# Attention and two MoE layers on one core: query tiles split half a step earlier, constants on a second queue, eight hidden-layer buffers instead of six

## The chip, the cores and the metric

The kernel runs on one core of one Trainium2 chip. The metric is device time in microseconds (us) of one execution; the time before is the median of three runs.

## The reference, cut to what matters

```python
scores = scale * np.matmul(q, k.transpose(0, 1, 3, 2))        # B,H,S,D = 2, 8, 576, 64
x = (np.log1p(np.abs(rel)) / psi_i)[..., None]                # rel = i - j
h = np.maximum(x @ w1 + b1, 0.0)                              # 32 hidden units
scores = scores + (h @ w2).transpose(2, 0, 1)[None]           # a bias for each head
attn = softmax(scores)
x = np.matmul(attn, v)                                        # as rows of 512, 1152 tokens
x = (x @ w_a) * (x @ w_b) @ w_out                             # first MoE block, d_ff 1536
x = (silu(x @ w_gate) * (x @ w_val)) @ w_out                  # second MoE block
```

## The kernel before, in words

The program is one stream: attention first, then the two MoE blocks, with one TensorE order written out by hand (`Pinned` keeps the matmuls in program order). A scheduler places the instructions of VectorE (DVE) and ScalarE (ACT) on their queues; which of the two engines gets a copy or a pass is settled at build time by `Share`, a running sum of estimated costs.

**The bias.** The class `Bias` makes the bias of all heads in 36 units of 16 rows. A unit has four passes (`passes`, L164): each makes a tile `hd` of up to 576 columns, relu(LW + bp), on DVE (L154) or ACT (L156). `LW` is the log table times w1; `bp` comes from the constants `cs`. `products` (L172) multiplies the four `hd` with w2 on TensorE into a bank `tp`, scales the result into a tile `bt` (L160 on DVE, L162 on ACT) and writes it to DRAM. `hd` has `HDS` buffers, so a pass may have to wait until TensorE has read the tile that had its buffer before.

**The attention.** A step is a pair of heads `p` and a block of rows `t`. The four steps of `t` = 4 come first and have one half each; the sixteen others have two halves (`b` = 0, 1) of 128 rows. Half `i` goes through three stages in three successive rounds of the loop at L472: `first(i)` makes the scores `ps` on TensorE (L319, in one PSUM tile of four banks), adds the bias and takes the maximum on DVE (`es`, L339) and the exponential on ACT (`es`, L345); `second(i-1)` transposes `es` into `ee`, copied out by ACT (L352) or DVE (L350); `third(i-2)` multiplies by the values (`pu`) and scales by the inverse sums (L408 to L411). After them stand the products of the bias units whose passes were issued at the top of the round. `MADE` (L36) says how many units a round has: eight in round 0, then 2, 1, 2, 1 and so on up to round 16. In a round with two units eight `hd` tiles are wanted.

**The query tiles.** The scores multiply in three terms, from a high part `qa` and a low part `qb` of the query tile: `split_q` (L230) makes `qa` (a cast on ACT, L212, or on DVE, L210) and then `qb` (a subtraction on DVE, L214) from `rawq`, which POOL's queue fetched earlier. Before the change the split for the next step is issued at the end of `first` of a step's last half (L451), so one half before its scores.

```python
            if 4 <= idx + 1 < len(steps) and (t == 4 or b == 1):
                heads.split_q(*steps[idx + 1])
```

**Queues.** SP's queue fetches `cs` (L138) and then `LW` (L139), later writes the bias and fetches MoE weights; POOL's queue fetches keys, queries, values and bias rows.

Of the kernel before, what the change touches and what calls it, by code (L numbers as in the profile page):

```python
# [34 lines left out]
FIRST = 4  # L35
MADE = (8, *(2, 1) * 8)  # L36
SCORED = 4
HDS, BTS, EES = 6, 6, 4


DFIX, DFAST, DSLOW = 160.0, 0.56, 1.04
# [34 lines left out]
class Activations:  # L76


    def __init__(self, pool):
        self.pool, self.late = pool, None  # L80
        self.acc = [pool.tile([P, NCC, CH], F32, tag=f"acc{c}", name=f"acc{c}") for c in range(2)]
        self.layer()
# [41 lines left out]
class Bias:  # L124
# [7 lines left out]
    def __init__(self, tc, stack, cst, lm, bias_d, heads, share):  # L132
        nc = self.nc = tc.nc
        self.tc, self.bias_d, self.share, self.pe, self.dve = tc, bias_d, share, Pinned(tc, nc.tensor), Pinned(tc, nc.vector)
        bc = self.bc = stack.enter_context(tc.tile_pool(name="bm", bufs=1, side="right"))
        cs = bc.tile([P, 214], F32, name="cs")
        LW = self.LW = bc.tile([P, S], F32, name="LW")
        nc.sync.dma_start(cs, cst)  # L138
        nc.sync.dma_start(LW, lm)  # L139
        one = bc.tile([P, 1], F32, name="one")  # L140
        nc.gpsimd.memset(one, 0.0)
        nc.scalar.activation(one, one, AF.Exp)
        W1, B1, self.W2, PS, self.RE = cs[:, 0:1], cs[:, 1:2], cs[:, 2:34], cs[:, 34:178], cs[:, 178:214]
        with tc.high_priority():
            bp = self.bp = bc.tile([P, 144], F32, name="bp")
            nc.vector.tensor_scalar(bp, PS, B1, None, op0=ALU.mult)
            ready = nc.vector.tensor_scalar(LW, LW, W1, None, op0=ALU.mult)
        heads.fetch_k(0)
        heads.fetch_first_q()
        heads.fetch_k(1)  # L150
# [151 lines left out]
def attention(ctx, tc, a4, heads, share, bias, units, bias_d, x, weights, ident):  # L302

    nc = tc.nc
    pe = units.pe
    with (
# [6 lines left out]
        def bias_rows(p, t, n):  # L313
            e = bias_d[t][:, 2 * p]
            return bass.AP(tensor=e.tensor, offset=e.offset + 15, ap=[[16 * H * BW, n // 16], [H * BW - 1, 16], [1, BW + S]])

        def scores(p, q, blocks, bt, sums):

            ka, kb = heads.got["k", p]  # L319
            qa, qb = q  # L320
            ps = ps2.tile([P, 2, 2, 512], F32, tag="big", name="ps")
            es = a4.tile([P, 2, S], F32, tag="es", name="es", bufs=3)
            for hf in range(2):
                for m, (lt, rt) in enumerate(((qa, ka), (qa, kb), (qb, ka))):
                    for j in range(2):
                        r = slice(64 * j, 64 * j + 64)
                        for n, (c0, b) in enumerate(blocks):
                            k0 = S * b + 288 * hf
                            pe.matmul(
                                ps[:, j, hf, :288], lt[r, c0 : c0 + P], rt[r, k0 : k0 + 288], start=m + n == 0, stop=m + n == len(blocks) + 1  # L330
                            )
            return ps, es, bt, sums

        def exponentials(ps, es, bt, sums, pinned):

            for j in range(2):
                nm = a4.tile([P, 1], F32, tag="nm", name="nm", bufs=4)
                least = (units.dve if pinned else nc.vector).tensor_tensor_reduce
                least(  # L339
                    out=es[:, j].rearrange("p (a j) -> p a j", a=2), in0=ps[:, j, :, :288], in1=bt[j].rearrange("p (a j) -> p a j", a=2),  # L340
                    op0=ALU.add, op1=ALU.min, scale=-0.125, scalar=3.0e38, accum_out=nm,
                )
                share.dve(S, 1.3)
                share.act(S, 190.0)
                nc.scalar.activation(es[:, j], es[:, j], AF.Exp, bias=nm, scale=-1.0, accum_out=sums[:, j : j + 1])  # L345
            return es.rearrange("p h k -> p (h k)")
# [77 lines left out]
        steps = [(p, t) for t in ORDER for p in range(H // 2)]  # L424
# [3 lines left out]
        def first(i):  # L428

            idx, p, t, b = halves[i]  # L430
            if b == 0:
                bt = a4.tile([P, BW + S], F32, tag="bias", name="bt", bufs=3)
                for r in range(1 if t < 4 else B):
                    n = P if t < 4 else 64
                    heads.queue.dma_start(bt[n * r : n * r + n], bias_rows(p, t, n))
                bt = [bt[:, BW * j : BW * j + S] for j in range(2)]
                if 0 < idx < 3:
                    heads.load_v(idx + 1, nc.sync)
                    heads.split_k(idx + 1)
                if 6 <= idx + 2 < len(steps):  # L440
                    heads.fetch_q(*steps[idx + 2])
                cells[idx] = bt, a2.tile([P, 4 if t < 4 else 2], F32, tag=f"sums{t < 4}", name="sums", bufs=3)
            bt, sums = cells[idx]
            blocks = [(P * b, b)] if t < 4 else [(64 * r, r) for r in range(B)]
            for made in range(MADE[0] if i == 0 else 1):
                if i == 0:
                    units.products(*units.passes(rest.pop(0)), bank)
                if made == SCORED * (i == 0):
                    live[i] = scores(p, heads.got["q", p, t], blocks, bt, sums[:, 2 * b : 2 * b + 2])
            live[i] = exponentials(*live[i], i == 0)  # L450
            if 4 <= idx + 1 < len(steps) and (t == 4 or b == 1):  # L451
                heads.split_q(*steps[idx + 1])

        def second(i):
# [17 lines left out]
        for i in range(len(halves) + 2):  # L472
            todo = [units.passes(rest.pop(0)) for _ in range(MADE[i] if 0 < i < len(MADE) else 0)]
            if i < len(halves):
                first(i)
            if 0 <= i - 1 < len(halves):
                second(i - 1)
            if i >= 2:
                third(i - 2)
            for unit in todo:  # L480
                units.products(*unit, bank)
            if i == len(MADE) - 1:
                bias.close()
                weights.pool = weights.pools[0] = ctx.enter_context(tc.tile_pool(name="wpa2", bufs=1, side="right"))
                weights.fetch(0, 0, 0)
                weights.fetch(0, 0, 1)
                ahead = chain(weights.words(0, 0, 0), weights.split(0, 0, 0), weights.words(0, 0, 1))
            if i > len(MADE) + 4:
                for op in islice(ahead, 1):
                    units.tc.keep_in_program_order(op)  # L490
# [230 lines left out]
```

## Time and profile before

| | us |
|---|---|
| median of 3 runs (652.32 to 652.73) | 652.34 |
| the profiled execution | 652.59 |
| its span in the trace | 650.5 |
| TensorE busy in the span | 617.5 (95%) |
| DVE busy | 535.8 (82%) |
| ACT busy | 344.6 (53%) |

The span is 2.1 us shorter than the profiled execution's own time. The busy shares are means over the whole span; attention, up to about 207.7 us, is a stage in which all three engines are busy, while in the MoE blocks ACT has little to do. The granted TensorE clock is 1.00 of full speed in all stretches.

### The profile page before, as it was taken

The page shows a single profiled execution, that of the slowest core. Times are in us where ns is not written, and L with a number is a line of the kernel's source. Part 1 is how long each engine was busy: PE and PEld are TensorE (multiplying, and loading weights), DVE is VectorE, ACT ScalarE, POOL GpSimd, SP SyncE. Part 2 cuts the span into 40 slices and gives each one's busy share as a digit, 9 for nine tenths or more (in the row PEclk, how much of TensorE's full clock was granted, in tenths as well). Part 3 has the DMA queues.
Part 4 walks back from the last instruction along what each step waited for, and adds up shares of the span by engine and source line. Part 5 has one row for each costly group of instructions (what it writes and reads, how often), then busy time and mean ns, then how long its engine had stood idle before and what let it go on. Part 6 is the DMA issues. An engine that isn't in the chain of part 4 may idle for free.

```text
span 650.5 us, 11312 instructions
## 1 busy us (share of the span) xinstructions
PE 617.5 (95%) x4470; PEld 554.9 (85%) x4470; DVE 535.8 (82%) x1033; ACT 344.6 (53%) x674; POOL 45.8 (7%) x66
## 2 busy tenths in 40 slices
PE   5879999999989989999999999999999999999997
PEld 2346565577778989999999999899999999999997
DVE  5968878778987899999899988997898988896452
ACT  5878888778786445544534332454555444433210
POOL 3210101011100000000000000450000000000000
PEclk9999999999999999999999999999999999999999
DMA  8884453573611331313313223111231313100012
GB/s 335 253 234 163 140 162 114 170 231 97 163 38 67 130 129 65 130 64 130 127 69 114 81 71 124 65 65 45 85 125 72 129 65 130 55 11 1 1 48 98
DMA packets 20996, 71.56 MB, mean 110 GB/s; under 512 B 5744, under 2 KB 7424, under 8 KB 16336
## 3 DMA queue, kind: packets, MB, share of 16 engines
q1 hardware_dynamic: 12672, 52.72, 22.5%
q0 software_dynamic: 8272, 18.13, 10.3%
q8 instruction: 35, 0.57, 0.4%
q14 instruction: 17, 0.14, 0.1%
HBM read 57.57 MB, written 13.25 MB: 109 GB/s over the span
## 4 chain that ended last, share of the span: by engine, by line
PE 77%; DVE 12%; ACT 7%; issue 2%; DMA 1%; POOL 0%; DVEq 0%; ACTq 0%; POOLq 0%
PE po L100 21%; PE pv L100 12%; PE pb L100 11%; PE tp L100 9%; PE pa L100 8%; PE pd L100 7%; PE pu L100 5%; PE ps L100 5%; ACT es L345 3%; ACT ee L352 1%; DVE es L339 1%; ACT hd L156 1%; DVE m L273 1%; DMA kr<-in_kd 1%; DVE hd L154 1%
## 5 line engine op out<-in xcount | busy, mean ns | idle before, releaser
L100 PE MATMUL po<-gh,woh 128*128 128x384 f32 x288 | 96.8, 336 | 1.4 <-DVE acc L597 1.3
L100 PE MATMUL po<-gl,woh 128*128 128x384 f32 x288 | 96.4, 335 | 1.2 <-DVE gl L532 1.2
L100 PE MATMUL po<-gh,wol 128*128 128x384 f32 x288 | 96.5, 335 | 0.0
L531 ACT CAST gh<-g 128x384 fp32r<-128x384 f32 x72 | 35.7, 514 | 85.6 <-DVE g L529 85.5
L100 PE MATMUL tp<-hd,cs 128*32 128x264 f32 (+17 forms) x352 | 49.3, 510 | 12.0 <-DVE hd L154 6.3
L339 DVE CUSTOM_DVE_ANT_0 es<-ps,bt 128x576 f32<-128x576 f32 x70 | 50.1, 753 | 10.7 <-PE ps L100 10.5
L345 ACT ACTIVATE es<-es,nm 128x576 f32<-128x576 f32 x72 | 55.8, 778 | 2.6 <-DVE nm L339 2.2
L100 PEld LDWEIGHTS po<-gh,woh 128*128 128x128 f32 x288 | 54.1, 188 | 2.3 <-DVE acc L597 2.3
L100 PEld LDWEIGHTS po<-gl,woh 128*128 128x128 f32 x288 | 54.1, 188 | 1.6 <-DVE gl L532 1.6
L100 PEld LDWEIGHTS po<-gh,wol 128*128 128x128 f32 x288 | 54.0, 188 | 0.0
L100 PE MATMUL pv<-x2h,wh 128*128 128x384 f32 x152 | 50.9, 335 | 0.0
L100 PE MATMUL pv<-x2l,wh 128*128 128x384 f32 x152 | 50.9, 335 | 0.0
L100 PE MATMUL pv<-x2h,wl 128*128 128x384 f32 x152 | 50.9, 335 | 0.0
L100 PE MATMUL tp<-ident,es 128*128 128x128 f32 x324 | 45.7, 281 | 2.5 <-ACT ee L352 1.8
L100 PE MATMUL pu<-ee,vv 128*64 128x128 f32 (+1 forms) x800 | 47.3, 267 | 0.0
L270 ACT ACTIVATE m<-raw 128x1024 f32<-128x1024 f32 x36 | 41.4, 1150 | 10.6 <-DVE wl L285 4.0
L100 PEld LDWEIGHTS tp<-hd,cs 128*32 128x32 f32 x352 | 13.9, 114 | 36.7 <-ACT hd L156 13.3
L284 ACT CAST wh<-m 128x1024 fp32r<-128x1024 f32 x24 | 25.3, 1053 | 37.0 <-PE pd L100 29.8
L273 DVE SCALAR_TENSOR_TENSOR m<-raw,m 128x1024 uint32<-128x1024 uint32 x36 | 44.5, 1238 | 0.2
L274 DVE SCALAR_TENSOR_TENSOR m<-raw,m 128x1024 uint32<-128x1024 uint32 x36 | 44.4, 1237 | 0.1
L100 PEld LDWEIGHTS pu<-ee,vv 128*64 128x64 f32 x800 | 39.3, 137 | 5.7 <-issue 5.2
L100 PEld LDWEIGHTS tp<-ident,es 128*128 128x128 f32 x324 | 34.5, 141 | 11.1 <-issue 4.8
(148 smaller groups left out, 1548.9 us busy)
## 6 DMA issues: line engine op xcount, KB each, us to landing
raw<-in_wm SPq DMA_DIRECT2D x36, 1024.0 KB, 4.8
bias_d<-bt SPq DMA_DIRECT2D x36, 295.5 KB, 5.5
bt<-bias_d POOLq DMA_DIRECT2D x16, 583.5 KB, 7.5
bt<-bias_d POOLq DMA_DIRECT2D x8, 291.8 KB, 10.2
kr<-in_kd POOLq DMA_DIRECT2D x4, 576.0 KB, 6.9
out_t<-acc SPq DMA_DIRECT2D x12, 192.0 KB, 1.9
rawq<-in_qd POOLq DMA_DIRECT2D x16, 128.0 KB, 3.0
vv<-in_vd SPq DMA_DIRECT2D x2, 640.0 KB, 7.5
```

The costliest lines, as they stand in the source:

```text
L100: return self.tc.keep_in_program_order(getattr(self.engine, name)(*args, **kwargs))
L154: self.last = self.nc.vector.tensor_scalar(dst, self.LW[:, :n], self.bp[:, m : m + 1], 0.0, op0=ALU.add, op1=ALU.max)
L156: self.nc.scalar.activation(dst, self.LW[:, :n], AF.Relu, bias=self.bp[:, m : m + 1])
L270: yield nc.scalar.activation(m, hi.bitcast(F32), AF.Abs)
L273: yield nc.vector.scalar_tensor_tensor(t, lo, 29, t, op0=ALU.logical_shift_right, op1=ALU.bitwise_or)
L274: yield nc.vector.scalar_tensor_tensor(t, hi, 0xC0000000, t, op0=ALU.bitwise_and, op1=ALU.bitwise_or)
L284: yield nc.scalar.copy(wh[:, :4], mt)
L339: least(out=es[:, j].rearrange("p (a j) -> p a j", a=2), in0=ps[:, j, :, :288], in1=bt[j].rearrange("p (a j) -> p a j", a=2), op0=ALU.add, ...
L345: nc.scalar.activation(es[:, j], es[:, j], AF.Exp, bias=nm, scale=-1.0, accum_out=sums[:, j : j + 1])
L352: nc.scalar.copy(dst, src)
L531: nc.scalar.copy(gh, g)
```

## The change

It has three parts. `split_q` of the next step is issued in `first` of a step's first half, one half earlier, and the first such split one step earlier. The fetch of `cs` goes to ACT's queue. `HDS` goes from 6 to 8.

```diff
-HDS, BTS, EES = 6, 6, 4
+HDS, BTS, EES = 8, 6, 4
...
-        nc.sync.dma_start(cs, cst)
+        nc.scalar.dma_start(cs, cst)
         nc.sync.dma_start(LW, lm)
...
             live[i] = exponentials(*live[i], i == 0)
-            if 4 <= idx + 1 < len(steps) and (t == 4 or b == 1):
+            if idx == 2:
+                heads.split_q(*steps[4])
+            if 4 <= idx < len(steps) - 1 and b == 0:
                 heads.split_q(*steps[idx + 1])
```

TensorE's, POOL's and (but for `cs`) SP's orders stay as they were. The scheduler orders DVE and ACT anew; the number of passes on each is the same (86 on DVE, 58 on ACT), and one copy of 128 columns goes from ACT to DVE. Three places follow.

The first is ACT's start: `hd` are the passes of the first units, `ka` the cast of the first keys, which has to wait for their fetch. Rows with - are of before, rows with + of the change.

```order
-L715 UNCONDITIONAL_BRANCH
+L717 UNCONDITIONAL_BRANCH
+L138 DMA cs<-in_cst 128x214
 L142 ACT_TABLE_LOAD
 L142 ACTIVATE one<-one 128x1
 L156 ACTIVATE hd<-LW,bp 128x528 x2
-L156 ACTIVATE hd<-LW,bp 128x544
+L156 ACTIVATE hd<-LW,bp 128x544 x2
 L212 CAST ka<-kr 128x1152
 L162 ACTIVATE bt<-tp,cs 128x63
-L156 ACTIVATE hd<-LW,bp 128x544
```

All four passes of the second unit (528 to 544 columns wide) now stand ahead of `ka`; the fourth stood behind it.

The second is DVE in round 5, between the two softmax pairs `es` (shown as ISA) of halves 4 and 5; the units there are 352 and 336 wide. Before:

```order
L339 ISA es,nm<-ps,bt 128x576
L339 ISA nm 128x1
L350 COPY ee<-tp 128x384
L160 TENSOR_SCALAR bt<-tp,cs 128x207
L350 COPY ee<-tp 128x384
L408 TENSOR_TENSOR acc_73<-pu,rc 128x128
L154 TENSOR_SCALAR hd<-LW,bp 128x352 x2
L411 TENSOR_TENSOR x0l<-acc_73,x0h 128x128
L154 TENSOR_SCALAR hd<-LW,bp 128x336
L160 TENSOR_SCALAR bt<-tp,cs 128x223
```

Of the change:

```order
L339 ISA es,nm<-ps,bt 128x576
L339 ISA nm 128x1
L210 CAST qa<-rawq 128x256
L160 TENSOR_SCALAR bt<-tp,cs 128x207
L350 COPY ee<-tp 128x384
L214 TENSOR_TENSOR qb<-rawq,qa 128x256
L390 COPY rc<-tp 128x128
L408 TENSOR_TENSOR acc_73<-pu,rc 128x128
L154 TENSOR_SCALAR hd<-LW,bp 128x336 x2
L411 TENSOR_TENSOR x0l<-acc_73,x0h 128x128
L154 TENSOR_SCALAR hd<-LW,bp 128x336
L160 TENSOR_SCALAR bt<-tp,cs 128x223
```

The passes of the first unit (352) have moved ahead of the earlier softmax pair, three of the second unit (336) stand in the gap, and the split of the next step's queries (`qa`, `qb`) stands there too, half a step before its use.

The third is ACT around the step whose scores start at 148.57 us, after the bias is done; `x1h` and `rw` belong to the end of a step, `m` to the first MoE weights. Before:

```order
L345 ACTIVATE es,sums<-es,nm 128x576
L352 COPY ee<-tp 128x384
L345 ACTIVATE es,sums<-es,nm 128x576
L212 CAST qa<-rawq 128x256
L410 CAST x1h<-acc_74 128x256
L383 COPY rw<-rs 128x256
L270 ACTIVATE m<-raw 128x1024
```

Of the change:

```order
L345 ACTIVATE es,sums<-es,nm 128x576 x2
L212 CAST qa<-rawq 128x256
L352 COPY ee<-tp 128x384
L345 ACTIVATE es,sums<-es,nm 128x576
L352 COPY ee<-tp 128x384
L345 ACTIVATE es,sums<-es,nm 128x576
L410 CAST x1h<-acc_74 128x256
L383 COPY rw<-rs 128x256
L270 ACTIVATE m<-raw 128x1024
```

The cast `qa` has moved ahead of the step's last pair of exponentials.

## Rows read from the trace of the kernel before

**Rows 1.** Busy time by stretch: stretch, length; busy PE, PEld, DVE, ACT, POOL; clock, DMA.
```profile
4.36:19.56 15.20, 11.41 (x80) 4.30 (x80) 11.40 (x22) 10.74 (x19) 2.23 (x4) 1.00 0.98 383
19.56:35.23 15.67, 13.29 (x107) 5.41 (x104) 14.51 (x32) 13.43 (x26) 4.31 (x7) 1.00 0.87 249
...
55.70:133.25 77.55, 71.55 (x781) 46.02 (x779) 62.12 (x178) 63.70 (x156) 8.10 (x13) 1.00 0.48 150
133.25:207.70 74.45, 69.38 (x808) 56.98 (x808) 60.82 (x170) 56.93 (x142) 7.93 (x13) 1.00 0.43 125
207.70:235.00 27.30, 25.63 (x145) 25.31 (x146) 24.07 (x36) 12.73 (x21) 0.00 (x0) 1.00 0.32 117
```

**Rows 2.** Waits, 36.7 to 133 us: engine, line, releaser, us in total, times, longest.
```profile
DVE hd L154 <- PE tp L100: 8.1, 8, 1.6
...
ACT hd L156 <- PE tp L100: 6.1, 7, 1.5
...
PE tp L100 <- ACT ee L352: 2.9, 6, 0.8
...
PE tp L100 <- ACT hd L156: 1.7, 4, 0.5
```

**Rows 3.** Waits of TensorE, 133 to 208 us, the same columns.
```profile
PE ps L100 <- ACT qa L212: 4.7, 5, 1.2
```

**Rows 4.** Timeline, the start: start us, us, engine, operation, [idle before <-releaser].
```profile
0.74 0.37 SPq L138 DMA_DIRECT2D cs<-in_cst  x1
...
1.17 0.42 SPq L139 DMA_DIRECT2D LW<-in_lm  x1
...
4.36 0.52 DVE L147 TENSOR_SCALAR LW<-LW,cs 128x576 f32<-128x576 f32 x1 [1.30 <-DMA LW<-in_lm]
...
8.67 1.15 ACT L212 CAST ka<-kr 128x1152 fp32r<-128x1152 f32 x1 [1.75 <-DMA kr<-in_kd]
...
11.87 0.50 DVE L160 TENSOR_SCALAR bt<-tp,cs 128x272 f32<-128x272 f32 x1 [0.66 <-PE tp L100]
...
14.68 0.96 DVE L214 TENSOR_TENSOR qb<-raw,qa 128x768 fp32r<-128x768 f32 x1 [1.46 <-ACT qa L212]
```

**Rows 5.** Timeline: the first softmax pair on DVE.
```profile
35.23 0.75 DVE L100 CUSTOM_DVE_ANT_0 es<-ps,bt 128x576 f32<-128x576 f32 x1
```

**Rows 6.** DMA issues of 22.1 to 22.6 us: bias rows, median us to landing.
```profile
bt<-bias_d POOLq DMA_DIRECT2D x2, 291.8 KB, 8.9
```

**Rows 7.** Timeline of TensorE: unit products of rounds 2 to 5, 15 and 16.
```profile
48.05 0.91 PE L100 MATMUL tp<-hd,cs 128*32 128x416 f32 x8
...
53.37 2.40 PE L100 MATMUL tp<-hd,cs 128*32 128x400 f32 x16
...
60.35 0.83 PE L100 MATMUL tp<-hd,cs 128*32 128x368 f32 x8
...
64.64 1.35 PE L100 MATMUL tp<-hd,cs 128*32 128x352 f32 x12
66.53 0.84 PE L100 MATMUL tp<-hd,cs 128*32 128x336 f32 x4 [0.53 <-ACT hd L156]
...
121.10 2.88 PE L100 MATMUL tp<-hd,cs 128*32 128x480 f32 x16
...
127.96 1.06 PE L100 MATMUL tp<-hd,cs 128*32 128x512 f32 x8
```

**Rows 8.** Timeline: the step whose scores start at 148.57 us.
```profile
148.13 0.39 ACT L212 CAST qa<-rawq 128x256 fp32r<-128x256 f32 x1
...
148.57 0.40 PE L100 MATMUL ps<-ka,qa 64*128 64x288 f32 x2 [0.88 <-ACT qa L212]
...
153.59 0.76 DVE L339 CUSTOM_DVE_ANT_0 es<-ps,bt 128x576 f32<-128x576 f32 x1 [1.48 <-PE ps L100]
```

**Rows 9.** Timeline of DVE, 163 to 177 us: the two rows with a wait.
```profile
163.06 0.29 DVE L408 TENSOR_TENSOR acc<-pu,rc 128x128 f32<-128x128 f32 x1 [0.47 <-PE pu L100]
...
176.60 0.76 DVE L339 CUSTOM_DVE_ANT_0 es<-ps,bt 128x576 f32<-128x576 f32 x1 [0.68 <-PE ps L100]
```

## The prediction

> **What bounds the kernel now.** I read the busy time by stretch first, then the waits, then the timeline where the waits stand. From 133 us on TensorE is the engine that is nearly full: it is busy 69.38 of 74.45 us in the last part of attention and 25.63 of 27.30 us where the MoE blocks begin [rows 1]. While the bias is made, from 55.70 to 133.25 us, it is busy 71.55 of 77.55 us, with DVE at 62.12 (80%) and ACT at 63.70 (82%) not far behind. In the start DVE sets the pace: up to the first softmax pair it is busy 11.40 of 15.20 and 14.51 of 15.67 us. So a gain can come from three places: DVE's waits in the start, TensorE's waits while the bias is made, and TensorE's waits after it. TensorE's order of work does not change, so what counts is when DVE and ACT deliver.
>
> The waits name the causes. Between 36.7 and 133 us DVE's passes `hd` waited 8 times, 8.1 us in all, until TensorE had read an older tile, and ACT's 7 times, 6.1 us [rows 2]. There are eight rounds with two units in that stretch (1, 3, ... 15), each wanting eight tiles where there are six buffers: the second unit's last passes wait for the first unit's products, and its products then wait for them. After 133 us TensorE's only frequent wait is for `qa` on ACT: 5 times, 4.7 us [rows 3].
>
> **The change, part by part.**
>
> *Constants on ACT's queue.* `LW` is issued at 1.17 us, behind `cs` at 0.74 [rows 4]; alone on SP's queue it can be issued at 0.74, so 0.43 us earlier. DVE waits for it 1.30 us after its work on `cs`, which is the most that could go; nothing goes if the transfer takes longer beside that of `cs`. I take 0.43, the issue slot, because that is the part that the rows show to be serial. ACT pays one issue ahead of its table load. I book nothing for it, since its first pass has to wait for `LW` anyway; if that cover were gone it would cost about 0.4 us (the issue of `cs` took 0.37). [...]
>
> *Eight buffers in the start.* ACT idles 1.75 us ahead of `ka` at 8.67 us, waiting for the keys [rows 4]. A fourth pass now stands in that gap, so that the second unit's products can follow the first's, and DVE's wait of 0.66 us at 11.87 for those products goes. `qb` at 14.68, which made DVE wait 1.46 us, now has five 576-wide passes ahead of it, and that wait goes too. Against it, 33 passes instead of 32 stand ahead of the first softmax pair on DVE: 0.39 us for 432 columns, an estimate from 0.52 us for 576. So 0.43 + 0.66 + 1.46 - 0.39 = **2.2 us**. At worst no wait goes and the pass is extra: -0.4. At best DVE loses all its idle time (3.80 + 1.16 us, rows 1), but the softmax at 35.23 [rows 5] needs bias rows that were issued at about 22.3 us and took 8.9 us [rows 6], so until 31.2: 4.0 us at most.
>
> *Eight buffers while the bias is made.* One unit takes TensorE 0.91 us at 416 columns, 0.83 at 368, 1.06 at 512 [rows 7]. Two units took 2.40 us in round 3, so 0.66 more than 0.91 + 0.83; from 64.64 to 67.37, so 2.73 us, in round 5, 1.07 more than twice 0.83; 2.88 in round 15, 0.76 more than twice 1.06. Part of this is counted as busy. The mean of the three, 0.83, over the eight rounds gives 6.6 us. With eight buffers all passes of both units are issued ahead of the round's softmax pair; in round 5 the second unit's three DVE passes now stand there and the first unit's one half earlier. What replaces the wait? With the six spells that lie in it taken off, the stretch of 77.55 us would be 72.6, DVE at 86% and ACT at 88%. That leaves room, but not enough for every wait to vanish, and the waits for `ee` on ACT (2.9 us, rows 2) have nothing to do with buffers. I take five sixths: **5.5 us**. The low end is the idle time that TensorE shows as a wait for `hd`, 1.7 us [rows 2]; the high end adds the waits for `ee`: 9.5.
>
> *Queries split half a step earlier.* At 148.57 us the scores wait 0.88 us for a cast that ACT began at 148.13, behind the two exponentials of the half before [rows 8]. In the new order it stands ahead of these. The scores can then follow TensorE's work, which ended at 147.69. All five waits go: 4.7 us. The moved work is the same two instructions on the same engines; it now stands ahead of the next half's softmax, where DVE waited 1.48 us for TensorE (153.59). Its fetch is issued a whole step before the split (L441), so I do not expect it to be late. In one step this cover is missing: from 163.06 to 176.60 DVE has no gap [rows 9], because the first MoE weights are converted there, so I take that step's 0.9 us off: **3.8 us**. Low end: the three waits from 163 us on bring nothing, so two times 0.88 or 1.7 us remain; high end: all idle time of TensorE there, 74.45 - 69.38 = 5.1 us.
>
> *MoE.* Its code is untouched and TensorE is busy 25.63 of 27.30 us at its start [rows 1]. DVE's order differs in places there. I book 0, and 1.7 us either way, the idle time that is there now.
>
> **The sum.** 2.2 + 5.5 + 3.8 = 11.5 us. The profiled execution took 652.59 us, so 641.1; the median of the runs is 0.25 below the profiled one, so **640.8 us**.
>
> **The rivals.**
>
> *The engines are full, not the buffers short.* DVE and ACT at 86 and 88% hand each wait on to the next instruction. Then the bias stage gives only its 1.7 us and the last stage its 1.7, with 2.2 from the start: 5.6, so 646.7 us. For it: the stretch without a gap on DVE [rows 9]. Against it: 8.1 us of DVE's idle time wait for exactly these buffers [rows 2]. Chance 0.20.
>
> *Given back at the start of MoE.* From 133.25 to 235 us DVE is busy 84.9 of 101.8 us. If its conversion of weights, rather than TensorE's arrival, sets when MoE gets going, the 3.8 us of the last stage are lost: 7.7 remain, 644.6 us. Against it: the conversion ran behind TensorE's release of tiles and should move with it. Chance 0.08.
>
> *Slower: work put ahead of the softmax.* Passes and splits that nobody waits for yet stand ahead of `es` on DVE. If two passes more are ahead of it in each of the eight rounds (0.32 us each at 352 columns, an estimate from 0.52 for 576, so 5.1 us), and `qb` (0.32, from 0.96 for 768 columns) in fifteen second halves (4.8 us), 9.9 us are lost against 2.2 + 3.8 gained: 656.2 us. It decides as soon as DVE's idle time ahead of `es` is smaller than what is put there. Against it: that idle time was 1.48 us after the bias stage [rows 8], and in round 5 three passes stand in the gap before and after. Chance 0.04.
>
> **The numbers.** My forecast has 0.66, the rivals 0.20, 0.08 and 0.04, and 0.02 is for no change. The low ends together would give 1.3 us of gain, the high ends 20.3; not all fall on one side. I set the range to gains of 4.3 to 18.8 us, 633.5 to 648.0 us, which takes in the first two rivals. About 0.2% (1.3 us) is what a measurement of this kernel can tell from no change. All cases but the last two are faster by more: faster 0.94, same 0.02, slower 0.04.
>
> **What would show it.** Right: TensorE's waits for `qa` after 133 us gone, DVE's waits of `hd` for TensorE under 2 us, two-unit rounds within 0.3 us of twice a one-unit round, the first softmax pair at about 33 us, the first MoE matmuls at about 196 us instead of 207.7. It would be wrong if the softmax rows `es` lost their waits for TensorE and TensorE waited for `es` or `ee` instead, or if MoE's stretch from its first matmul on grew by more than 1.7 us.

## The result

| | before | after |
|---|---|---|
| median (4 runs each, same chip) | 652.33 us | 644.83 us |
| lowest to highest | 652.11 to 652.73 | 644.35 to 645.35 |
| profiled execution, its span | 652.59, 650.5 | 645.35, 643.5 |

The ratio is 0.9881 (95% interval 0.9868 to 0.9895), a gain of 7.5 us. The forecast was 640.8, in a range of 633.5 to 648.0: the sign and the range held, the gain was two thirds of the 11.5 us.

Four stages split the span of the profiled execution at moments that TensorE's own order fixes: the first scores of the second half, those of the nineteenth half (the expectation of the filled gap counts from 0 and calls it the eighteenth), and the first MoE matmul (all in us of the trace).

| stage | before | after | difference | forecast |
|---|---|---|---|---|
| start, to the second half's scores | 36.81 | 33.59 | -3.2 | -2.2 |
| bias stage, to the nineteenth half | 96.44 | 94.41 | -2.0 | -5.5 |
| rest of attention, to MoE | 74.38 | 72.17 | -2.2 | -3.8 |
| MoE | 442.87 | 443.33 | +0.5 | 0 |

So the start gave more than was booked, and the bias stage and the rest of attention gave less. The border cuts through one term: the first of the five waits for `qa`, 0.87 us, ends at 133.25 us, so it lies in the bias stage here, while the forecast booked it under the rest of attention. Counted as the forecast has it, the bias stage gave 1.2 us of 5.5, and the rest 3.1 of 3.8.

The busy times of after by stretch answer to [rows 1] (stretch, length; busy PE, PEld, DVE, ACT, POOL; granted clock, DMA share, GB/s):

```profile
33.59:52.55 18.96, 17.74 (x222) 13.07 (x223) 12.39 (x42) 14.65 (x39) 4.19 (x7) 0.91 0.80 217
52.55:128.00 75.45, 67.58 (x783) 46.03 (x779) 61.50 (x181) 63.15 (x150) 8.27 (x14) 0.98 0.49 153
128.00:200.17 72.17, 68.39 (x810) 56.63 (x808) 61.14 (x169) 58.94 (x147) 6.50 (x12) 1.00 0.49 127
200.17:227.50 27.33, 25.66 (x148) 25.34 (x147) 24.27 (x36) 13.02 (x22) 0.00 (x0) 1.00 0.32 116
```

What is new is the granted clock, 0.91 and 0.98 where it was 1.00. From the fifth to the nineteenth half TensorE now idles more, 7.87 us of 75.45 against 6.00 of 77.55 before, and DVE and ACT have hardly filled up: 82 and 84% instead of 80 and 82.

The waits of after between 33.5 and 128 us answer to [rows 2] (engine, line, releaser, us in total, times, longest):

```profile
DVE hd L154 <- PE tp L100: 6.6, 6, 2.9
...
ACT hd L156 <- PE tp L100: 5.7, 6, 2.6
PE tp L100 <- ACT ee L352: 5.6, 7, 1.2
...
PE ps L100 <- DVE nm L100: 3.8, 1, 3.8
...
PE tp L100 <- ACT bt L162: 1.9, 2, 1.5
PE tp L100 <- DVE bt L160: 1.6, 2, 1.1
```

No wait of TensorE's matmuls for `hd` is left; they wait for banks to be emptied instead, 5.6 us for `ee` (2.9 before) and 3.5 us for `bt` (1.0 before). The passes still wait for TensorE, nearly as long as before, but nobody waits for them. After 128 us the waits of TensorE, to be held against [rows 3], are

```profile
PE tp L100 <- ACT ee L352: 2.8, 4, 1.0
PE ps L100 <- DVE nm L339: 0.5, 2, 0.3
PE tp L100 <- ACT rw L383: 0.3, 1, 0.3
```

`qa` is gone, and `ee` has come in its place. The unit products, to be held against [rows 7], show the buffers at work (timeline of TensorE, rounds 3, 4, 5 and 15):

```profile
51.10 1.52 PE L100 MATMUL tp<-hd,cs 128*32 128x400 f32 x16
57.53 0.82 PE L100 MATMUL tp<-hd,cs 128*32 128x368 f32 x8
61.84 1.36 PE L100 MATMUL tp<-hd,cs 128*32 128x352 f32 x16
...
118.15 1.84 PE L100 MATMUL tp<-hd,cs 128*32 128x480 f32 x16
```

Two units now take less than twice one. Over the eight two-unit rounds their products took 21.2 us before and 12.2 after: 9.0 us saved, more than the 6.6 that three sampled rounds had promised. So the mechanism worked, and the time was lost elsewhere.

Where the clock fell is seen in windows of TensorE (busy us, granted clock, DMA share, GB/s), after:

```profile
32.00:34.00 2.00, 0.41 (x4) 0.94 1.06 364
34.00:36.00 2.00, 2.00 (x21) 0.50 1.08 322
36.00:38.00 2.00, 2.00 (x17) 0.71 0.87 235
86.00:88.00 2.00, 0.70 (x4) 1.00 0.74 232
88.00:90.00 2.00, 2.00 (x17) 0.59 0.67 217
90.00:92.00 2.00, 2.00 (x20) 0.56 0.48 151
```

Twice TensorE had little to do, 0.01 us of work from 29.8 to 33.59 us and 0.70 between 86 and 88, and both times the granted clock was 0.50 of full speed just behind, from 34.0 to 37.0 us and from 88.4 to 91.5. In the start, the rows of after (start us, us, operation, [idle before]) are

```profile
4.32 0.29 DVE L146 TENSOR_SCALAR bp<-cs 128x144 f32<-128x144 f32 x1 [4.32 <-DMA cs<-in_cst]
4.52 0.60 DVE L147 TENSOR_SCALAR LW<-LW,cs 128x576 f32<-128x576 f32 x1
...
11.27 0.50 DVE L160 TENSOR_SCALAR bt<-tp,cs 128x272 f32<-128x272 f32 x1
...
13.98 0.95 DVE L214 TENSOR_TENSOR qb<-raw,qa 128x768 fp32r<-128x768 f32 x1
...
32.01 0.75 DVE L100 CUSTOM_DVE_ANT_0 es<-ps,bt 128x576 f32<-128x576 f32 x1
```

Against [rows 4]: the waits of 0.66 and 1.46 us ahead of `bt` and `qb` are gone. But `cs`, on ACT's queue, now lands at 4.3 us (`bp`, its first user, began at 2.76 before), and the work on `LW` began at 4.52 instead of 4.36. The first softmax pair came at 32.01 instead of 35.23 [rows 5].

### The profile page after: what moved, and what is told of

Same layout as the page of the kernel before. It is cut to its first block, busy times and chain, and to the rows that moved or that the text cites. A ratio compares the mean times of both kernels' runs of the same rounds, so it can differ in the third digit from the quotient of the medians.

```text
span 643.5 us, 11334 instructions
## 1 busy us (share of the span) xinstructions
PE 606.4 (94%) x4470; PEld 553.4 (86%) x4470; DVE 535.0 (83%) x1034; ACT 346.2 (54%) x673; POOL 45.6 (7%) x66
## 4 chain that ended last, share of the span: by engine, by line
PE 70%; DVE 17%; ACT 9%; issue 3%; DMA 1%; POOL 0%; ACTq 0%; DVEq 0%; POOLq 0%
PE po L100 20%; PE pv L100 12%; PE pb L100 10%; PE pa L100 7%; PE tp L100 7%; PE pd L100 6%; PE pu L100 5%; PE ps L100 3%; ACT hd L156 2%; ACT es L345 2%; DVE m L274 2%; DVE m L273 2%; ACT bt L162 2%; ACT ee L352 1%; DVE es L339 1%
## 5 line engine op out<-in xcount | busy, mean ns | idle before, releaser
L533 ACT CAST gh<-g 128x384 fp32r<-128x384 f32 x72 | 35.9, 514 | 88.5 <-DVE g L531 88.4
L100 PE MATMUL tp<-hd,cs 128*32 128x264 f32 (+17 forms) x352 | 36.7, 495 | 11.8 <-DVE hd L154 6.0
L534 DVE TENSOR_TENSOR gl<-g,gh 128x384 fp32r<-128x384 f32 x72 | 38.9, 552 | 5.1 <-ACT gh L533 5.0
```

The lines of the kernel that those rows point to most:

```text
L100: return self.tc.keep_in_program_order(getattr(self.engine, name)(*args, **kwargs))
L533: nc.scalar.copy(gh, g)
L534: nc.vector.tensor_tensor(gl, g, gh.bitcast(F32), op=ALU.subtract)
```

## The experiments

All twelve were timed beside the kernel before. First, each part by itself and two together. My first theory was an *exchange*: buffers let passes for later rounds stand ahead of the `ee` copies, for which TensorE then waits. The rival was that the engines are simply full.

**The split alone** (`HDS` = 6, `cs` on SP's queue as before).

```diff
-HDS, BTS, EES = 8, 6, 4
+HDS, BTS, EES = 6, 6, 4
-        nc.scalar.dma_start(cs, cst)
+        nc.sync.dma_start(cs, cst)
```

> Only the earlier split of the query tiles; six buffers, constants on SP's queue. If the split alone removes TensorE's five waits for qa and nothing takes their place, the time is 4 to 5 us under before (about 648). If the wait only moves on, to the copies ee or to DVE in the steps that convert weights, it is 2 us or less (650 to 651). The eight two-unit rounds should keep their waits for hd.

Measured: 646.93 us (646.88 to 647.15), ratio 0.991 (0.9897 to 0.9922), 6.0 us below before and so more than the waits for `qa` alone. **Eight buffers alone** (the change's `split_q` lines and the `cs` line undone):

> Only eight buffers. Theory: the waits for hd go (6 to 7 us), but ACT and DVE then work on the next round's passes ahead of the copies ee, TensorE waits there, and the clock drops once or twice after a long gap, so that only 2 to 5 us remain (647 to 650), and the five waits for qa stay. Rival: the waits for ee in the full change come from the split standing between the passes; then here they are not larger than in before, and the time is 6 us or more under it.

Measured: 647.93 us (646.70 to 649.22), ratio 0.9925 (0.9909 to 0.994), in the band of the theory; TensorE's waits for `ee` between 30 and 134 us are 3.9 us instead of 2.9, so the split is not what makes them. **The constants alone**:

```diff
-        nc.sync.dma_start(cs, cst)
+        nc.scalar.dma_start(cs, cst)
```

> Only the constants on ACT's queue. Theory: their landing is later (4.3 instead of 2.8 us, as in the full change), DVE's first work with them too, so the start is 0.2 to 0.4 us later and the time at most that much longer. Rival: the issue slot of 0.43 us is won and the time is shorter by that.

Measured: 654.37 us (652.11 to 655.76), ratio 1.002 (1.0008 to 1.0032): slower, if anything. From issue to landing `cs` took 3.7 us instead of 2.0, TensorE's first product came at 5.80 us instead of 5.46, and the second half's scores 0.72 us later than before. **Split and buffers without the constants**:

> The change without the constants' move. Theory: 0.2 to 0.5 us faster than the full change (644.3 to 644.6). Rival: the start is set by other work and the time is that of the full change within 0.1 us; if it is slower by 0.4 us, the constants' move was worth its issue slot.

Measured: 644.88 us (644.60 to 646.36), ratio 0.9882 (0.9869 to 0.9895), like the whole change, as the rival had it. In its profiled execution, the slowest of the four, the first softmax had to wait for the bias rows:

```profile
34.29 0.76 DVE L100 CUSTOM_DVE_ANT_0 es<-ps,bt 128x576 f32<-128x576 f32 x1 [2.66 <-DMA bt<-bias_d]
```

What follows: the split alone gives 6.0 us and the buffers alone 5.0, together 8.1. They overlap. The rest of attention answers to the split alone (72.16 us with it, 74.40 with the buffers alone). The bias stage was 96.44 us before, 93.73 with the split, 94.18 with the buffers and 93.09 with both, but each of these three has a fall of the clock behind the first softmax, which with both (33.7 to 40.5 us, so 6.8) lasts twice as long as in the others (about 3.4 us). The stretch from the third to the nineteenth half has none in any of the four, so there they can be compared (us; the products are those of its seven two-unit rounds):

| | stretch | products | TensorE's waits for `ee` and `bt` |
|---|---|---|---|
| before | 89.69 | 18.4 | 3.1 |
| split alone | 85.45 | 18.2 | 1.3 |
| buffers alone | 87.09 | 10.5 | 6.8 |
| both | 85.69 | 10.5 | 8.3 |

Beside the split, the buffers shorten the products there by 7.7 us, and all of it comes back: the stretch is no shorter. What they add to the split is won before it, in the start (33.59 us in the whole change, 35.87 with the split alone) and in the first two-unit round (1.68 us instead of 2.81).

Next, three that vary the order and the number of buffers; all have the split and `cs` on SP's queue. **Passes behind the copies**:

```diff
-            todo = [units.passes(rest.pop(0)) for _ in range(MADE[i] if 0 < i < len(MADE) else 0)]
             if i < len(halves):
                 first(i)
             if 0 <= i - 1 < len(halves):
                 second(i - 1)
+            todo = [units.passes(rest.pop(0)) for _ in range(MADE[i] if 0 < i < len(MADE) else 0)]
```

> The split and the eight buffers of the change with the constants as before, and the ReLU passes of each round written after the copies of the transposes instead of ahead of the scores, so that they stand behind the `ee` copies on ACT and DVE. Beside the same kernel without that edit (644.9 us, gain 8.1). Order theory (the eight buffers let passes for later rounds stand in front of the `ee` copies and TensorE then waits for those): the waits of TensorE for ACT's `ee` between 36 and 134 us fall from 8.2 us in 11 to under 3, DVE's and ACT's `hd` waits for TensorE come back in part, and the middle stage gets 1 to 3 us shorter: 642 to 644 us. Rival, engines full (ACT and DVE have no more to give there whatever the order): the waits change name, the middle stage stays within 0.7 us of 93.1, 644.2 to 645.6 us. Second rival, the passes come too late (TensorE then waits for ReLU passes before the products): TensorE waits for `hd` for over 4 us, 646 to 649 us.

Measured: 643.76 us (643.12 to 644.97), ratio 0.9871 (0.9858 to 0.9884). TensorE's waits for `ee` between 30 and 134 us fell from 5.4 us to 3.8 (the 8.2 of the text are those of all attention), and from the third half to the nineteenth, where neither kernel has a fall of the clock, the stretch took 84.80 us instead of 85.69. So the order of passes and copies is worth 0.9 us there. That is less than the exchange theory asked for (1 to 3 us, and waits under 3): the time fell in its band, but the waits for `bt` grew from 3.5 to 4.4 us, as the rival had it. **Copies first**:

```diff
-                keep(ee[:, 3 * k : 3 * k + 3], tp, 3 * P)
+                with tc.high_priority():
+                    keep(ee[:, 3 * k : 3 * k + 3], tp, 3 * P)
```

> The split and the eight buffers with the constants as before, and the `ee` copies given precedence over the ReLU passes on the engines that make them (the passes keep their place in the program). Beside the same kernel without that edit (644.9 us). Order theory: TensorE's waits for `ee` between 36 and 134 us fall from 8.2 us to under 3 and 1 to 3 us of them are won: 642 to 644 us. Rival, engines full: the idle time of TensorE comes back under other names (`hd`, `bt`, `nm`) and the time stays at 644.2 to 645.6 us. Both give the same part after 208 us within 1 us, since no product is made there.

Measured: 645.28 us (643.88 to 647.26), ratio 0.9897 (0.9878 to 0.9915), no difference. It decides little: the waits for `ee` between 30 and 134 us were 5.6 us instead of 5.4, so the edit hardly moved the copies. **Seven buffers**:

```diff
-HDS, BTS, EES = 8, 6, 4
+HDS, BTS, EES = 7, 6, 4
```

> The split of the change with the constants as before and seven buffers for the ReLU passes instead of six (646.9 us) or eight (644.9 us). If what the buffers bring is a wait of a pass for the buffer of the round but one before, each buffer brings about its share: 645.5 to 646.3 us. If only a full round of four passes ahead counts (8 = 2 x 4), seven is like six: 646.4 to 647.4 us. If the gain of the eighth buffer is already given back as waits for `ee`, seven is as good as eight or better: 643.8 to 645.2 us.

Measured: 645.51 us (644.58 to 646.34), ratio 0.9895 (0.9881 to 0.9908). By the number this is the first case, a share for each buffer; the stages don't bear it out. From the third to the nineteenth half it took 86.40 us, against 85.45 with six buffers and 85.69 with eight, and its profiled execution shows no fall of the clock at all (bias stage 92.80 us) where those with six and with eight do. That made me take the clock as the next suspect.

**The gap filled.** TensorE gets four products to do in the 3.78 us before the second half's scores (their result is used by nothing); otherwise it is the changed kernel.

```diff
+                if i == 1:
+                    filler = bank()
+                    for _ in range(4):
+                        pe.matmul(filler[:, :464], ident, units.LW[:, :464], start=True, stop=True)
                 if made == SCORED * (i == 0):
```

> The changed kernel with four more matrix products (128x128 by 128x464, their result is used by nothing) in the gap of 3.78 us that TensorE has before the scores of the second half, so that it is at work when the first softmax pair frees their bank. Clock theory (the drop of the granted clock to 0.5 behind this gap stretches the 24 score products from 1.8 to 3.1 us and the transposes after them): no granted clock under 0.9 between 32 and 40 us, the last score product of that half starts within 1.6 us of the first instead of 2.4, and the half after it begins 1 to 1.7 us earlier beside its own first scores; the whole 643 to 644.2 us if nothing gives it back, 644.8 if the next wait takes it. Rival (the drop does not come from the idle time, or the longer score products lie beside other work): the clock drops there all the same, or it does not and the stretch to the eighteenth half is no shorter: 644.3 to 645.5 us. If the filling ends after the bank is free the scores start late by what it overruns.

Measured: **640.90 us** (640.81 to 642.96), ratio 0.9832 (0.9817 to 0.9847), 3.9 us below the change and below every case that was written down. The timeline of TensorE, the changed kernel first, then the filled one:

```profile
33.59 0.75 PE L100 MATMUL ps<-ka,qa 64*128 64x288 f32 x4 [3.78 <-DVE nm L100]
...
36.67 1.42 PE L100 MATMUL tp<-ident,es 128*128 128x128 f32 x9
...
39.13 1.68 PE L100 MATMUL tp<-hd,cs 128*32 128x448 f32 x16 [0.80 <-ACT ee L352]
```

```profile
30.32 3.35 PE L100 MATMUL tp<-LW,ident 128*128 128x464 f32 x8 [0.44 <-ACT bt L162]
33.61 0.54 PE L100 MATMUL ps<-ka,qa 64*128 64x288 f32 x4
...
35.40 1.20 PE L100 MATMUL tp<-ident,es 128*128 128x128 f32 x9
...
36.90 1.69 PE L100 MATMUL tp<-hd,cs 128*32 128x448 f32 x16
```

The scores begin at the same time. From there to the transposes it is 3.08 us in the one and 1.79 in the other, and the transposes take 1.42 and 1.20: 1.5 us by the clock, which stays at 1.00 in every window of the filled kernel. Another 0.80 us is a wait for `ee` that the scheduler, counting on the fuller TensorE, arranged away. And the second fall, near 88 us, is gone as well, 1.6 us by the next run. 1.5 + 0.8 + 1.6 make the 3.9 us by which the bias stage is shorter (90.50 instead of 94.41).

The next two tell filling from its side effects. **A short fill**: one product of 64 columns at the beginning of the gap, so that most of the gap stays (2.85 us of idling ahead of the scores).

```diff
-                    for _ in range(4):
-                        pe.matmul(filler[:, :464], ident, units.LW[:, :464], start=True, stop=True)
+                    for _ in range(1):
+                        pe.matmul(filler[:, :64], ident, units.LW[:, :64], start=True, stop=True)
```

> The changed kernel with one short product (128x128 by 128x64, used by nothing) at the beginning of TensorE's gap of 3.78 us ahead of the scores of the second half, so that the gap stays over 3 us. Clock theory: the granted clock falls to 0.5 behind it as in the changed kernel, the 24 score products take about 3.1 us, and the time is 644.0 to 645.5 us. Rival (what the four filling products won came from anything else than filling the time, the allocation of a bank or the order of the copies): 640.5 to 642.5 us.

Measured: 643.98 us (643.52 to 647.26), ratio 0.9872 (0.9853 to 0.9892). The first fall is there (0.50 from 34 to 36 us), as the clock theory had it, and no execution of this kernel is without one by its mean clock (0.997 four times, 0.995 once; the filled kernel has 1.00 in three of four). The second isn't in the profiled execution, though up to that place the two executions agree within 0.02 us from the fifth half on. TensorE's timeline there, the changed kernel first, then this one:

```profile
87.85 0.55 PE L100 MATMUL tp<-ident,es 128*128 128x128 f32 x3 [0.99 <-ACT ee L352]
88.23 0.60 PE L100 MATMUL tp<-ident,rw 128*128 128x128 f32 x2
88.76 2.40 PE L100 MATMUL pu<-ee,vv 128*64 128x128 f32 x20
91.09 1.13 PE L100 MATMUL tp<-hd,cs 128*32 128x368 f32 x8
92.16 0.40 PE L100 MATMUL ps<-ka,qa 64*128 64x288 f32 x2
```

```profile
87.85 0.55 PE L100 MATMUL tp<-ident,es 128*128 128x128 f32 x3 [1.01 <-ACT ee L352]
88.23 0.43 PE L100 MATMUL tp<-ident,rw 128*128 128x128 f32 x2
88.59 1.31 PE L100 MATMUL pu<-ee,vv 128*64 128x128 f32 x20
89.84 0.83 PE L100 MATMUL tp<-hd,cs 128*32 128x368 f32 x8
90.59 0.40 PE L100 MATMUL ps<-ka,qa 64*128 64x288 f32 x2
```

The same waits, the same work, and 1.57 us between them: that is what one fall costs here, and the bias stage is 92.82 us instead of 94.41. **The kernel before, filled** with three such products:

```diff
+                if i == 1:
+                    filler = bank()
+                    for _ in range(3):
+                        pe.matmul(filler[:, :464], ident, units.LW[:, :464], start=True, stop=True)
                 if made == SCORED * (i == 0):
```

> The kernel of before with three filling products (128x128 by 128x464, used by nothing) in its gap of 2.76 us ahead of the scores of the second half. The granted clock does not fall there in its profile, so by the clock theory there is nothing to win: 651.8 to 653.0 us, no difference. Rival (the filling gains by the order that it brings about on ACT, where the first copies of the transposes come together ahead of the next exponentials): 649.5 to 651.3 us.

Measured: 650.41 us (650.05 to 651.05), ratio 0.9963 (0.995 to 0.9975). The time is in the rival's band, 2.3 us below before, and ACT's timeline shows a part of it:

```profile
38.03 0.86 ACT L352 COPY ee<-tp 128x384 f32<-128x384 f32 x2 [0.72 <-PE tp L100]
38.78 0.79 ACT L345 ACTIVATE es<-es,nm 128x576 f32<-128x576 f32 x1
```

Both copies now stand ahead of the next exponentials; before, one exponential stood between them, and TensorE waited 0.80 us for the second. The second to the third half's scores took 5.97 us instead of 6.75, so the order is worth 0.8 us. A second part is the clock after all. A profiled execution with one fall has a mean clock of 0.997 (the short fill); all five executions of this kernel have 1.00, and eight of the nine of the kernel before that were timed beside it have 0.997 or less. Of the 46 executions of the kernel before that were timed beside the experiments 35 do, and took 653.0 us on average, the other 11 652.0. So by its mean clock the kernel before falls too, in most executions though not in its profiled one, and the filling takes away that 1 us as well. The remaining half microsecond stays open. (The start is 1.16 us shorter in the trace, but DVE and ACT have the same order there as before: that is the one execution, not the edit.)

Last, two that look for a faster kernel. **Late passes and a filled gap** (the two edits above together, `cs` on SP's queue):

> The kernel with the late passes (split, eight buffers, constants as before, ReLU passes written behind the copies; 643.8 us) with the four filling products (used by nothing) ahead of the scores of the second half. Clock theory: no granted clock under 0.9 between 30 and 40 us, the second half takes 1.4 to 2.3 us less than its 7.8, and the whole is 641.3 to 642.4 us; if the late passes and the filling are worth in full what they were each worth alone beside the kernel without them (1.1 and 3.9 us beside the change), 639.3 to 641.0. Rival (what the clock loses is found again in the next wait): 643.2 to 644.4 us.

Measured: 641.52 us (640.97 to 643.38), ratio 0.983 (0.9815 to 0.9845). The clock theory's band held, the sum of both gains did not come: with the gap filled, the late passes bring next to nothing more (bias stage 90.57 us, 90.50 without them). TensorE's waits for `ee` between 30 and 134 us fall again, from 4.8 to 3.0 us beside the next kernel, but those for `bt` rise from 3.6 to 5.7. **The filled kernel with `cs` on SP's queue**:

```diff
-        nc.scalar.dma_start(cs, cst)
+        nc.sync.dma_start(cs, cst)
```

> The changed kernel with the four filling products (used by nothing; 640.9 us) and the constants fetched on SP's queue ahead of the log table, as before: the two differ by the place of that one fetch alone. If the fetch on ACT's queue wins the 0.43 us of the prediction's first term, this one is slower: 641.1 to 641.8 us. If it costs the 0.2 to 0.7 us by which the first products began later where it alone was moved, this one is faster: 640.2 to 640.8 us. Clock theory: no granted clock under 0.9 behind the filling in either, and from the second half's scores to the first of the MoE within 1 us of the 162.6 us of the other. A landing of the bias rows later than the first scores (as in the split and eight buffers without it, 34.29 us) would make the filling end before the scores and cost up to 2 us: 641 to 643.

Measured: 641.11 us (640.10 to 642.18), ratio 0.9817 (0.98 to 0.9835): no difference from the filled kernel. TensorE's first product comes 0.34 us earlier (5.37 against 5.71), but the bias rows don't:

```profile
32.98 0.76 DVE L100 CUSTOM_DVE_ANT_0 es<-ps,bt 128x576 f32<-128x576 f32 x1 [1.43 <-DMA bt<-bias_d]
```

With eight buffers the first softmax comes at 32.0 us at the earliest, in eight of nine profiles by 33.0, and in all six with `cs` on SP's queue it waited for its rows, by 0.33 to 2.66 us; in these six the bias rows fetched before 34 us took 10.1 to 11.3 us from issue to landing (medians). What the constants do ahead of that is hidden.

## Why the forecast was right in sign and four microseconds off

**The start: -3.2 instead of -2.2.** The waits of 0.66 and 1.46 us went as forecast. The term of 0.43 us for the constants was wrong in sign: `LW` did land 0.2 us earlier (3.4 us after an issue at 0.74 instead of 3.2 after one at 1.17), but `cs`, which the work on it needs too, took 1.6 us longer on ACT's queue (3.6 instead of 2.0). The forecast had asked how long `LW` would take beside `cs`, not `cs` beside `LW`. So the move did not save even the time of issuing: `cs` landed at 4.3 us instead of 2.7, and DVE could begin on `LW` only then. The first softmax came 1.0 us earlier than the sum had it, near the floor that [rows 6] had given, the landing of the bias rows. That 1.0 us is luck of the execution that was read: two others with six buffers and the same order of DVE and ACT up to there had the second half's scores at 35.87 us (the split alone) and 35.65 (before, filled) instead of 36.81, and the wait of 0.66 us was 0.19 and 0 in them. Against these two the start won 2.1 to 2.3 us.

**The bias stage: -2.0 instead of -5.5.** With the wait for `qa` taken out it is -1.2. Two steps failed. The first is one that the forecast never took: it priced every matmul at the clock of [rows 1], 1.00, and asked only when DVE and ACT deliver. In the profiled execution two falls of the clock cost 1.5 + 1.6 = 3.1 us, the first behind a gap of 3.78 us (2.76 before), the second behind two waits close together at 86 to 88 us (0.45 and 0.99). The filled gap shows the first one's price, the short fill the second one's. That the first one comes of the gap is shown for the changed kernel, since the filling removed it and the short product did not (1.00 against 0.50 from 34 to 36 us); what brought on the second is not shown, since the short fill has the same waits without it. Without the falls the stage would have given about 4.3. In the medians the falls weigh less, because most executions of the kernel before have one too, at about 1 us.

The second is the five sixths. The gross was 9.0 us, not 6.6. The three sampled rounds were like the others (1.1 us saved in each); the yardstick was too long, because two units back to back take less than twice one (1.36 us in round 5, not twice 0.83). And of the 9.0 some 4.3 net were left, with the split's help: about half, not five sixths. The two errors go against each other, and it is luck that their product, 5.5, lies no further from 4.3. The rest came back as waits for banks (`ee` 5.6 instead of 2.9 us, `bt` 3.5 instead of 1.0). Full engines, the first rival, would have left the stage a gain of 1.7 us; without the falls it is two and a half times that. But for the buffers beside the split the rival's words fit: from the third half on, all that they took off the products came back as other waits. That DVE and ACT are full isn't shown: they are busy 81 and 86% in the filled kernel's stage (73.73 and 77.61 of 90.50 us), and the late passes still won 0.9 us with the same work (0.3 with the gap filled). So the exchange theory is a small part of it, and what holds that stretch at about 85 us stays open. The 0.8 us that the order of the filled kernels won is no part of what came back, since that wait of 0.80 us for `ee` stands in the kernel before as well.

The credit was misplaced too. The forecast gave the whole bias stage to the buffers, but the split alone shortens it by 2.7 us, 0.9 of that the wait for `qa` (without its one fall of the clock, at 1.5, it would be 4.2), and its two-unit rounds are no faster: 21.0 us of products against 21.2. Part of what it does there is seen in TensorE's waits between 36.8 and 133 us, 1.8 us for `ee` and 0.2 for `hd` against 2.9 and 1.7 [rows 2]. Two parts that ease the same queues are not to be added.

**The rest of attention: -2.2 instead of -3.8.** With the fifth wait for `qa` counted in, it is -3.1. All five went, as forecast, but the forecast asked only what is late next on DVE. ACT was late next. Its timeline, before and after, and then TensorE's after:

```profile
149.04 1.13 ACT L270 ACTIVATE m<-raw 128x1024 f32<-128x1024 f32 x1
150.34 0.48 ACT L352 COPY ee<-tp 128x384 f32<-128x384 f32 x1 [0.16 <-PE tp L100]
```

```profile
143.57 1.16 ACT L270 ACTIVATE m<-raw 128x1024 f32<-128x1024 f32 x1
144.62 0.86 ACT L352 COPY ee<-tp 128x384 f32<-128x384 f32 x2
```

```profile
145.15 0.44 PE L100 MATMUL tp<-ident,rw 128*128 128x128 f32 x2 [0.81 <-ACT ee L352]
```

The conversion `m` of MoE's first weights stands ahead of the copies in both, and starts 0.8 us after the exponentials in both. Before, TensorE's wait for `qa`, 0.88 us [rows 8], hid it: ACT was done with `m` before the transposes were, and waited 0.16 us for them. Now TensorE comes that much earlier, finds ACT still at `m`, and waits 0.81 us for the copies. There are four such waits, 2.8 us in all where one of 0.4 stood before; three of them stand behind a conversion of 1024 columns on ACT (1.04 to 1.16 us). So 2.4 us of the four `qa` waits in this stage (3.9 us) came back, which leaves 1.5 of the 2.2 us; the other 0.7 was not traced. No run tried to move these conversions.

**MoE: 0.** It was 443.33 us instead of 442.87, inside the 1.7 us either way; over all the kernels it lay between 442.5 and 443.6.

**The signs.** `qa` gone, the softmax near 33 us and two-unit rounds within 0.3 us of twice one: right. DVE's `hd` waits under 2 us: wrong (6.6), but harmless, since with eight buffers a pass that waits for a tile is one that nobody needs yet. The first MoE matmul came at 200.17, not 196; in the filled kernel, without the falls, it came at 196.25. The warning sign came up: DVE's waits of `es` for TensorE went from 10.5 us to 2.3, and TensorE waited for `ee` instead, for a part of the gain and not for all.

## What to carry to other kernels

Price a change by the clock it leaves as well as by the waits it removes: here TensorE ran at 0.50 of full speed behind one wait of 3.78 us and behind two of 0.45 and 0.99 close together, and the profiled execution with a few useless products in the long gap had neither fall, about 3 us of clock (1.5 and 1.6). When a wait goes, look at what it hid: the queue that the next wait hangs on may be as long as before, and then the wait only moves on. A mechanism can work in full (9.0 us of products saved here) and give nothing where the next wait takes it. Before a difference of a microsecond in one stage is explained, look at a second execution with the same order there. Parts that ease the same stretch are to be tried one by one, because their gains overlap.

## What was not expected of the hardware

The same idle time did not give the same clock here. Ahead of the second half's scores TensorE idled 2.76 us in the kernel before and 2.79 with seven buffers, and the granted clock stayed at 1.00; with the split alone it idled 2.76 us as well, and the scores ran at 0.50. Near 88 us the changed kernel and the short fill have the same waits within 0.02 us, and only one of them fell. What decides between them, no run here shows. Of the four executions of the filled kernel three had a mean clock of 1.00 and took 640.81 to 640.99 us, and one had 0.997, the mean of an execution with one fall, and took 642.96: for a single run of this kernel, that is a difference of about 2 us, as much as the buffers add to the split (646.93 to 644.88).
